# A new written order and engine choice for a linear-attention and feed-forward kernel

## The chip, the cores and the metric

The kernel runs on one core of a Trainium2 chip. A core has a matrix engine (TensorE, PE in the profile), three engines for elementwise work (VectorE or DVE, ScalarE or ACT, GpSimd or POOL), a queue engine (SyncE or SP) that issues all of this kernel's data transfers, and sixteen DMA engines that carry them out. The engines run at the same time, each works through its own instructions in order, and they wait for one another by semaphores. The metric is the device time of one execution in microseconds; less is better.

## The reference

The inputs r, k, v, w have 4 batches, 8 heads, 768 steps and 48 elements per head, in float32. For each batch and head a state S of 48 x 48 is carried along the steps:

```
y[t] = r[t] . (S + (u * k[t]) v[t]^T)
S    = diag(w[t]) S + k[t] v[t]^T
```

The outputs y, put together over the heads, are 3072 tokens of 384 elements. A feed-forward block follows: h = x @ w_in (384 x 2048), g = s * relu(h)^2 + b, out = g @ w_out (2048 x 384), in float32.

## The kernel before

The steps are cut into 24 chunks n of 128 steps (six per batch). Within a chunk the recurrence is written as matrix products. With the running sum of log w (a product with a triangular matrix), r and k are scaled by its exponentials; then the chunk's own part is a masked 128 x 128 product per head, and the part from earlier chunks a product with the carried state. The first four chunks are "packed": two neighbouring chunks of a batch are loaded together and take several smaller products each. Two chunks make one tile T of 256 tokens for the feed-forward block, twelve tiles in all.

Each piece of work is an operation with a short name. n is a chunk, T a tile, i a part.

| name | engine | what it does (line) |
|---|---|---|
| load n.x, li, lo, load_u, small | SP | loads of w, r, k, v (x = 0 to 3; L296, packed L304), of the pieces of w_in and w_out (L719, L729), of u, s, b |
| ln, exp, exn | ACT | log of w; exponentials of the running sums, E (L317, L413, L428) |
| cum, inc | PE, DVE | running sums into a PSUM tile cums (L372 to L397), and inc = cums + log w (L418) |
| mul | DVE | prd = r, k times E (L437, L444) |
| tr, tev | PE, ACT | transposes of prd and their copy RK to SBUF (L471, L491); for chunks 9 and up tev is a DMA transpose on SP (L501) |
| mt, msk | PE, DVE | K R^T of two chunks in four PSUM buffers (L531, L543), masked into mt_sb, two msk a chunk (L555) |
| rkp, rku, cd, yd | POOL, DVE for cd | the u term: r*k, times u, summed per head, times v (L322, L328, L345, L351) |
| vb | POOL or ACT | v to bfloat16 (L870, L872) |
| ymm, yev | PE, DVE | y of the chunk (L574 to L606), plus yd, into x_sb (L651) |
| dmm, sup, l2, st | PE, DVE, POOL | the state's update (L625, L638, L671, L679, L458, L688) |
| xtr, xev | PE, ACT | x transposed, copied into the tile's xT (L699, L714) |
| g1 T.i, relu, sq | PE, ACT, DVE or ACT | an eighth of h (six matmuls, L749), relu (L762), square into gT (L772 on ACT, L774 on DVE) |
| g2 T.i, oev, store | PE, DVE, SP | four matmuls into the output tile o_ps (L793), times s plus the b term (L804), store (L823) |
| ci, co, csred, csadd, cssplit, csspread, csevac | several | weights to bfloat16 (ci, co: L870 on ACT, L874 on DVE, L872 on POOL); column sums of w_out for the b term |
| u_mm, u_ev | PE, DVE | u spread over the partitions (L893, L897) |
| +N | PE | N matmuls on a constant tile, whose result is not used (L1119) |

Nothing is scheduled by a framework. The text ORDER lists all operations once, and the last loop of the kernel emits them in this order. Each engine's queue is ORDER's words for that engine, in their sequence. A suffix picks the engine where there is a choice: @A is ACT, @D is DVE, @P is POOL.

```
for o in pl.order(ORDER):
    if isinstance(o, int):
        warm(o)
    else:
        o["fn"](*o["args"])
```

The method order (L138) checks that each operation comes after those it needs and after the last user of the buffer that it takes. The planned durations given to add (the third argument) are read by a search that is not part of the kernel; they decide nothing when the kernel is built.

Buffers are taken in rings, in ORDER's sequence. PSUM has six buffers "P", which cum, tr, mt (four at once), ymm, xtr, dmm and g1 take in turn, and two buffers "o" for o_ps: the output tile that comes next but one waits until oev has read the earlier one. The w_in and w_out pieces share four staging buffers: a lo waits for the ci that has read its buffer.

Of the kernel before, what the change touches and what calls it, by code (L numbers as in the profile page):

```python
# [1159 lines left out]
```

## Time and profile before

| what | value |
|---|---|
| median of 13 runs | 186.88 us (185.64 to 195.22) |
| profiled execution | 185.64 us, its span 183.6 us |
| PE busy | 176.3 us, 96% of the span |
| DVE busy | 140.4 us, 77% |
| ACT busy | 146.5 us, 80% |
| POOL busy | 104.7 us, 57% |
| mean granted clock of TensorE | 0.999 |
| first g1 starts | 20.89 us |
| last matmul ends | 180.4 us |
| g1 matmuls (L749) | 576, 71.9 us |
| g2 matmuls (L793) | 400, 72.8 us |

The span reaches from the first to the last instruction; the run's time holds some more around it. Busy times add up an engine's instructions without the overlaps, so a share of 96% means that PE has 7.3 us without a matmul. In a timeline line the first number is the start, the second the time until the last instruction of the line ends, then engine, line, operation, the tiles, their shapes and the number of instructions; a bracket tells how long the engine was idle before it and whose end it waited for. Matmuls of one line overlap, and so do neighbouring instructions of DVE and ACT, so that costs in a queue are better read from start to start.

### The profile page before, as it was taken

What the parts mean: (1) busy time and instruction counts of PE and PEld (TensorE: products, weight loads), DVE (VectorE), ACT (ScalarE), POOL (GpSimd) and SP (SyncE); (2) the same over time, 40 slices, a digit from 0 to 9 for tenths busy, and PEclk for the clock granted to TensorE, in tenths of its full rate; (3) what the DMA queues carried; (4) which work ended last, traced back from release to release, by engine and by line L of the source; (5) the groups of instructions that cost most, each with busy time, mean ns of one, the idle gap of its engine ahead of it and who ended that gap; (6) DMA issues with size and microseconds to landing.
All of it is one profiled execution on the core that took longest, in us unless ns stands there. A gap on an engine that the chain in (4) does not pass through costs nothing.

```text
span 183.6 us, 5087 instructions
## 1 busy us (share of the span) xinstructions
PE 176.3 (96%) x1994; PEld 139.5 (76%) x1994; DVE 140.4 (77%) x250; ACT 146.5 (80%) x286; POOL 104.7 (57%) x139
## 2 busy tenths in 40 slices
PE   7999899999998999997999999999999999999993
PEld 4568798866786787785788878877886978888672
DVE  7659899998969979859978698697898959522231
ACT  3588999999989999887878979878989677754900
POOL 3685930019988999698397299194495493100000
PEclk9999999999999999999999999999999999999999
DMA  6999989589989989999699989999994890004022
GB/s 162 324 312 345 407 294 327 116 154 230 217 174 210 219 181 215 201 238 151 127 221 188 188 201 185 202 234 192 199 193 97 191 190 4 2 5 171 0 86 86
DMA packets 113449, 34.14 MB, mean 186 GB/s; under 512 B 108177, under 2 KB 111378, under 8 KB 113426
## 3 DMA queue, kind: packets, MB, share of 16 engines
q1 hardware_dynamic: 113426, 33.83, 80.6%
q8 instruction: 15, 0.25, 0.6%
q14 instruction: 8, 0.07, 0.1%
HBM read 25.17 MB, written 4.72 MB: 163 GB/s over the span
## 4 chain that ended last, share of the span: by engine, by line
PE 47%; ACT 3%; DVE 2%; issue 0%; ACTq 0%
PE o_ps L793 21%; PE h_ps L749 19%; PE mt_ps L543 2%; DVE mt_sb L555 2%; PE y_ps L606 1%; ACT rh L762 1%; PE xt_ps L699 1%; PE y_ps L597 1%; ACT gT L772 1%; PE d_ps L638 1%; PE cums L391 1%; DVE o_sb L804 1%; ACT E L428 0%; ACT xT L714 0%; DVE inc L418 0%; ACT E L413 0%
## 5 line engine op out<-in xcount | busy, mean ns | idle before, releaser
L793 PE MATMUL o_ps<-w_out,gT 128*128 128x384 bf16 (+1 forms) x400 | 72.8, 320 | 1.5 <-DVE gT L774 0.9
L749 PE MATMUL h_ps<-xT,w_in 128*128 128x256 bf16 x576 | 71.9, 273 | 0.2
L762 ACT ACTIVATE rh<-h_ps 128x512 bf16<-128x512 f32 x96 | 55.4, 599 | 14.2 <-PE h_ps L749 13.0
L749 PEld LDWEIGHTS <-w_in 128*128 128x128 bf16 x576 | 61.8, 114 | 4.3 <-issue 0.2
L793 PEld LDWEIGHTS <-gT 128*128 128x128 bf16 x400 | 36.6, 98 | 19.1 <-DVE gT L774 1.5
L772 ACT ACTIVATE gT<-rh 128x512 bf16<-128x512 bf16 x69 | 42.3, 633 | 0.3
L351 POOL TENSOR_TENSOR yd<-vt,cd 128x384 bf16<-128x384 f32 x20 | 19.0, 954 | 17.1 <-DVE cd L345 17.1
L555 DVE TENSOR_TENSOR mt_sb<-mt_ps,tri_strict 128x512 bf16<-128x512 f32 x40 | 25.3, 680 | 2.7 <-PE mt_ps L543 2.7
L328 POOL TENSOR_TENSOR rku<-rkp,u_bc 128x384 f32<-128x384 f32 x24 | 24.2, 1008 | 0.7
L322 POOL TENSOR_TENSOR rkp<-rkt 128x384 f32<-128x384 f32 x20 | 23.9, 1198 | 0.9 <-DMA rkt<-in_k_dram 0.9
L804 DVE SCALAR_TENSOR_TENSOR o_sb<-o_ps,s_bc,bconst 128x384 f32<-128x384 f32 (+1 forms) x25 | 14.8, 594 | 11.7 <-PE o_ps L793 11.7
L774 DVE TENSOR_TENSOR gT<-rh 128x512 bf16<-128x512 bf16 x27 | 15.7, 590 | 9.2 <-ACT rh L762 9.1
L444 DVE TENSOR_TENSOR prd<-rkt,E 128x768 bf16<-128x768 f32 x20 | 22.1, 1108 | 0.1
L413 ACT ACTIVATE E<-cums 128x388 f32<-128x388 f32 (+1 forms) x32 | 15.7, 496 | 6.2 <-DVE inc L418 3.3
L688 POOL TENSOR_TENSOR st<-stmp,l 128x384 bf16<-128x384 bf16 x16 | 15.6, 979 | 6.4 <-DVE stmp L679 6.4
L872 POOL CAST vb<-vt 128x384 bf16<-128x384 f32 x12 | 7.4, 624 | 17.9 <-DMA vt<-in_v_dram 17.9
L651 DVE TENSOR_TENSOR x_sb<-y_ps,yd 128x384 bf16<-128x384 f32 x24 | 13.0, 551 | 3.7 <-PE y_ps L606 2.1
L345 DVE TENSOR_REDUCE cd<-rku 128x8 f32<-128x384 f32 x24 | 12.9, 543 | 1.6 <-POOL rku L328 1.6
L714 ACT COPY xT<-xt_ps 128x384 bf16<-128x384 bf16 x24 | 11.0, 482 | 2.3 <-PE xt_ps L699 2.2
L418 DVE TENSOR_TENSOR inc<-cums,logw 128x384 f32<-128x384 f32 x16 | 8.8, 549 | 4.2 <-ACT E L413 3.4
L317 ACT ACTIVATE logw<-wt 128x384 bf16<-128x384 f32 x20 | 10.5, 523 | 0.2 <-DMA wt<-in_w_dram 0.2
L679 DVE TENSOR_TENSOR stmp<-d_ps,st 128x384 bf16<-128x384 f32 x16 | 8.7, 549 | 2.0 <-PE d_ps L638 1.6
(94 smaller groups left out, 198.9 us busy)
## 6 DMA issues: line engine op xcount, KB each, us to landing
out_dram<-o_sb SPq DMA_DIRECT2D x23, 192.0 KB, 2.7
wt<-in_w_dram SPq DMA_DIRECT2D x20, 192.0 KB, 3.8
rkt<-in_r_dram SPq DMA_DIRECT2D x20, 192.0 KB, 4.1
rkt<-in_k_dram SPq DMA_DIRECT2D x20, 192.0 KB, 3.7
vt<-in_v_dram SPq DMA_DIRECT2D x20, 192.0 KB, 3.8
wi_st<-in_moe_w_in_dram SPq DMA_DIRECT2D x4, 768.0 KB, 9.0
wo_st<-in_moe_w_out_dram SPq DMA_DIRECT2D x4, 768.0 KB, 7.2
pkt<-in_w_dram SPq DMA_DIRECT2D x2, 384.0 KB, 4.1
```

The source lines that it names most:

```text
L322: nc.gpsimd.tensor_tensor(out=rkp, in0=c["r"], in1=c["k"], op=ALU.mult)
L328: nc.gpsimd.tensor_tensor(out=rku.rearrange("t h d -> t (h d)"), in0=c["rkp"].rearrange("t h d -> t (h d)"), in1=u_bc, op=ALU.mult,)
L351: nc.gpsimd.tensor_tensor(out=yd, in0=c["v"], in1=c["cd"].unsqueeze(2).to_broadcast([128, H, D]), op=ALU.mult,)
L413: nc.scalar.activation(out=c["E"][:, x, 0:w], in_=ps[:, 0:w], func=AF.Exp)
L444: nc.vector.tensor_tensor(out=prd[:, :, :, 0:D], in0=c["rk"], in1=c["E"][:, :, 0:HD].rearrange("t x (h d) -> t x h d", h=H), op=ALU.mult,)
L555: nc.vector.tensor_tensor(out=c["mt"][:, sg], in0=c["mt_ps"][sg], in1=(masks[:, n % 2] if packed(n) else tri_strict) .unsqueeze(1) .to_bro ...
L749: nc.tensor.matmul(ps[:, f, :], lhsT=w_in_sb[ft // FPP][:, kt, :].rearrange("p (m j) -> p j m", j=FPP)[:, ft % FPP, :], rhs=xT[T][:, kt, : ...
L762: nc.scalar.activation(out=rh, in_=hs[T, i], func=AF.Relu)
L772: nc.scalar.activation(out=g, in_=rh, func=AF.Square)
L774: nc.vector.tensor_tensor(out=g, in0=rh, in1=rh, op=ALU.mult)
L793: nc.tensor.matmul(os_[T, k][:, cols], lhsT=gT[T][:, ft, tt * 128 : (tt + 1) * 128], rhs=w_out_sb[ft // FPP][:, ft % FPP, cols], start=(ft ...
L804: nc.vector.scalar_tensor_tensor(out=o_sb[:, cols], in0=os_.pop((T, k))[:, cols], scalar=s_bc, in1=bconst[:, cols], op0=ALU.mult, op1=ALU.add,
```

## The change

The whole text ORDER is replaced by another order of the same operations. It holds 40 of the unused matmuls instead of 38. Some operations stand on other engines: among the weight casts, ci1 moves from ACT to DVE and ci2 from DVE to POOL; vb4, vb5 and vb7 move from POOL to ACT, vb9, vb10 and vb13 from ACT to POOL; 70 of the 96 squares are on ACT instead of 69. The planned cost of u_mm is 0.85 instead of 0.7; the search that made the new order also counted the instruction fetches as work of the DMA engines, and let only one engine at a time read a PSUM tile. No function, shape, buffer count or dependency changes.

```
--- before.py
+++ after.py
 ORDER = """
-load0.0 load0.1 load_u ln0 ln1 +16 cum0.0 cum0.1 cum1.0 exp0.0 load0.2 exp0.1 mul0.0 mul0.1 exp1.0
-load0.3 mul1.0 cum1.1 load2.0 load2.2 load2.3 u_mm tr0 exp1.1 mul1.1 +2 tr1 u_ev tev0 tev1 +9 mt0
-vb0@P load4.0 l20 rkp0 rku0 load2.1 rkp1 l21 msk0.0 msk1.0 vb1@A ln2 msk0.1 rku1 li0 ln3 cd0 +4
-cum2.0 exp2.0 dmm0 cum3.0 msk1.1 cum3.1 ln4 vb2@A cum2.1 sup0 exp3.0 exp2.1 vb3@A st0 +1 cum4.0 li1
-exp3.1 l22 yd0 mul2.0 mul2.1 exp4.0 mul3.0 ymm0 cd1 mul3.1 yd1 ymm1 dmm1 tr2 sup1 rkp2 l23 ci0@A
-yev0 dmm2 tev2 tr3 li2 rku2 sup2 yev1 xtr0 tev3 cd2 +5 xtr1 l24 rkp3 xev0 rku3 yd2 xev1 +1 mt2 g10.0
-ci1@A msk2.0 st2 msk2.1 msk3.0 li3 g10.1 relu0.1 msk3.1 relu0.0 dmm3 g10.2 g10.3 relu0.2 lo0 ymm2
-ci2@D cd3 ymm3 lo1 st1 yd3 lo2 sup3 yev2 cum4.1 xtr2 ci3@A relu0.3 g10.4 load5.0 sq0.0@D lo3 load5.1
-yev3 load6.0 load4.1 sq0.3@A g10.5 co0@D load4.2 xev2 xtr3 load5.2 csred0@D sq0.2@A sq0.1@A relu0.4
-g10.6 xev3 exp4.1 small2 g20.4 g20.0 g10.7 load4.3 g11.0 g11.1 co1@D relu0.5 g11.2 sq0.5@A relu0.7
-relu0.6 sq0.4@D sq0.7@A csred1@D sq0.6@A ln5 small g11.3 relu1.0 vb4@P load5.3 rkp4 csadd1@D relu1.2
-relu1.3 g20.1 g11.4 cum5.0 relu1.1 exp5.0 co2@D csred2@D g20.5 cum5.1 exp5.1 sq1.2@A csadd2@D
-load6.1 load6.2 g11.5 co3@D sq1.0@D g11.6 csred3@D csadd3@D load7.0 cssplit g11.7 g20.2 g20.6 g20.3
-rku4 mul4 relu1.4 load8.0 sq1.3@A ln6 load9.0 relu1.6 relu1.7 sq1.1@A cum6.1 g20.7 relu1.5 csspread
-load6.3 mul5 tr4 cum6.0 load7.1 tr5 csevac sq1.5@A l25 oev0.1 oev0.0 exp6.0 tev5 exp6.1 dmm4 g21.4
-g21.0 tev4 g21.1 g21.5 vb5@P sup4 sq1.4@A cd4 dmm5 mul6 mt4 rkp5 load7.2 ln7 load7.3 g21.6 sup5
...
-rkp7 sup6 exn8 load10.1 g12.1 inc9 exp9.0 oev1.1 relu2.0 sq2.0@A g12.2 relu2.1 dmm7 tr7 rku7 g12.3
-tev7 relu2.2 rkp6 sq2.1@D oev1.0 load11.3 vb8@P cd7 sup7 mul8 load9.2 g12.4 g22.0 relu2.3 relu2.4
...
-g14.1 g14.2 g14.3 cd10 relu4.0 exp13.0 inc13 sup11 mul12 l212 cd11 oev3.0 relu4.1 yd10 vb12@P mt10
-relu4.2 g14.4 g23.7 relu4.3 sq4.0@D sq4.1@A load13.3 load14.1 exn13 st10 load13.2 msk10.0 msk11.0
-load15.0 oev3.1 rkp12 l213 msk10.1 relu4.4 ln14 g14.5 store2.0 load16.0 g24.4 st11 msk11.1 sq4.2@A
-cum14.0 g24.0 dmm12 rku12 sq4.4@A g14.6 yd11 sup12 mul13 ymm10 ymm11 yev10 ln15 rkp13 relu4.5
-exp14.0 sq4.3@A load15.3 yev11 relu4.6 sq4.5@A vb13@A g14.7 g24.1 g24.5 rku13 tev12 load14.2 inc14
...
-relu7.7 sq7.7@A store5.1 relu8.0 mt18 tev20 exn21 msk19.0 relu8.1 msk18.0 msk18.1 yd19 g27.6 g18.2
-ln22 msk19.1 g18.3 cum22.0 dmm18 g27.2 sq8.1@A ln23 inc22 mul21 g27.3 ymm19 g18.4 g27.7 relu8.3
-relu8.2 rkp20 sq8.0@A load22.2 g18.5 tev21 sq8.3@A yev19 relu8.4 exp22.0 rku20 yd18 vb21@P rkp21
-sup18 relu8.5 ymm18 xtr19 rku21 st18 sq8.2@A exn22 cum23.0 sq8.4@D g18.6 oev7.1 yev18 oev7.0 xtr18
-g18.7 g28.0 inc23 store7.0 relu8.6 g28.4 load20.3 g28.5 cd21 xev18 exp23.0 xev19 supn21 supn20
-sq8.5@A relu8.7 load23.2 mt20 store6.1 g19.0 mul22 g19.1 g28.1 msk20.0 msk20.1 msk21.0 yd21 msk21.1
...
-relu11.3 sq11.2@A sq11.0@A relu11.6 store9.1 g210.5 relu11.7 g210.0 g210.6 g210.7 store8.1 store9.0
-g210.1 relu11.4 sq11.3@A g210.2 store8.0 sq11.6@D sq11.7@D oev10.1 g210.3 sq11.4@D g211.8 g211.0
-g211.1 oev10.0 store10.1 g211.2 g211.4 g211.3 g211.5 g211.6 g211.7 g211.9 g211.10 g211.11 oev11.0
-oev11.1 oev11.2 store10.0 store11.1 store11.0 store11.2
+load0.0 ln0 ln1 +17 cum0.0 load0.1 load0.2 load_u cum1.0 cum0.1 exp0.0 rkp0 u_mm cum1.1 load0.3
+mul0.0 load2.3 exp1.0 exp0.1 l20 vb1@A exp1.1 load2.2 load2.0 mul0.1 mul1.0 load2.1 +4 tr0 load4.0
+mul1.1 +5 tr1 u_ev l21 tev0 vb0@P rku0 tev1 dmm0 +5 mt0 ln2 cd0 sup0 msk1.0 ln3 vb3@A rkp1 yd0 rku1
+li0 +1 cum2.0 cum3.0 st0 msk0.0 msk1.1 msk0.1 rkp3 exp2.0 mul2.0 l22 cum2.1 +5 cum3.1 ln4 ymm0 cd1
+exp2.1 exp3.0 exp3.1 ci0@A yd1 mul2.1 yev0 cum4.0 vb2@A ymm1 xtr0 xev0 li2 mul3.0 exp4.0 tr2 tev2
+li1 mul3.1 +2 dmm2 yev1 li3 lo0 dmm1 xtr1 xev1 sup2 tr3 sup1 +1 g10.0 ci2@P tev3 g10.1 mt2 load5.0
+ci1@D relu0.0 lo1 relu0.1 g10.2 rku3 g10.3 cd3 sq0.0@A sq0.1@A lo2 relu0.2 relu0.3 ci3@A st2 msk2.0
+lo3 g10.4 msk2.1 small2 msk3.0 l24 relu0.4 rkp2 cum4.1 load6.0 g10.5 msk3.1 ymm3 load4.1 rku2 ymm2
+sq0.3@D cd2 st1 yd3 yev3 yd2 co0@D l23 xtr3 yev2 g10.6 csred0@D load4.2 exp4.1 relu0.5 ln5 g20.4
+cum5.0 load5.1 sq0.2@A xtr2 relu0.6 xev2 co1@D load5.2 g10.7 xev3 csred1@D rkp5 small g20.0 g11.0
+load6.1 exp5.0 sq0.4@A g11.1 sq0.5@A relu0.7 rkp4 g11.2 cum5.1 g11.3 sq0.6@A csadd1@D co2@D load6.2
+relu1.0 relu1.1 csred2@D load4.3 g20.5 g20.1 relu1.2 sq0.7@A sq1.2@A exp5.1 csadd2@D co3@D csred3@D
+g20.6 csadd3@D g20.2 g11.4 g20.7 g11.5 cssplit load5.3 load7.0 g11.6 relu1.3 rku4 sq1.0@A sq1.3@A
+ln6 sq1.1@A mul4 relu1.4 relu1.5 sq1.5@D mul5 g20.3 cum6.0 relu1.6 csspread load8.0 cum6.1 csevac
+exp6.0 dmm3 tr4 g11.7 tr5 exp6.1 tev4 tev5 load6.3 oev0.1 g21.0 vb4@A sq1.4@A oev0.0 load9.0 sup3
+relu1.7 g21.4 rku5 vb5@A sq1.6@A load7.1 load8.1 ln7 mt4 mul6 g21.1 l25 g21.5 dmm4 g21.6 load7.2
...
+g12.2 oev1.0 rku6 sq2.0@A mul7 g12.3 oev1.1 rkp7 sup6 relu2.1 sq2.1@D tr7 cum9.0 rku7 inc9 vb7@A cd6
+load10.0 dmm7 st6 relu2.3 relu2.2 tev7 exp9.0 sup7 mul8 cd7 g12.4 relu2.4 g22.0 g12.5 mt6 msk6.0
...
+load13.3 g23.3 oev3.0 g14.0 g14.1 relu4.0 mt10 sq4.0@A relu4.1 g14.2 load15.3 relu4.2 load15.1
+load14.1 yd10 msk10.0 rkp11 rku11 l212 rkp13 rku13 msk10.1 cd11 msk11.0 g14.3 cum13.0 g14.4 msk11.1
+exp13.0 load14.2 sq4.1@A relu4.3 inc13 g23.7 load12.3 yd11 ymm10 g24.0 oev3.1 g14.5 ymm11 yev10
+store2.0 load17.0 sq4.3@A ln14 load15.2 relu4.4 exn13 relu4.5 sq4.2@A g14.6 xtr10 relu4.6 xev10
+yev11 sq4.4@D mul12 xtr11 xev11 g14.7 g24.1 relu4.7 g24.4 rkp12 cum14.0 g24.5 vb13@P tev12 ln15
...
+load19.0 load17.3 g25.6 sup15 yev13 cd15 xtr13 cd14 dmm14 sup14 mt14 msk14.0 xev13 msk14.1 st15 st14
+yd15 yd14 g25.3 g16.0 g16.1 relu6.0 g16.2 g16.3 msk15.0 load17.1 relu6.1 msk15.1 ymm14 ymm15 sq6.0@D
+l216 rkp16 ln18 relu6.2 mul16 g16.4 vb16@P g16.5 yev15 yev14 relu6.3 xtr15 cum18.0 g25.7 oev5.0
...
+g18.6 inc22 sq8.4@A mul21 sq8.3@D mt18 tev21 exn22 st19 rku19 load21.3 store6.1 g28.5 sq8.5@A g28.1
+supn21 cd19 msk19.0 g28.6 msk18.0 relu8.6 g18.7 sq8.6@A msk18.1 ln23 ymm18 msk19.1 yd19 rkp21 yev18
+relu8.7 ymm19 vb20@P cum23.0 g28.2 yd20 rku21 inc23 yev19 mt20 cd21 xtr19 store7.1 store6.0 load22.1
+load23.1 load22.2 load23.2 msk20.0 msk21.0 sq8.7@A store7.0 load22.3 yd21 vb21@P st18 exp23.0 xtr18
+msk20.1 supn20 g28.7 msk21.1 xev18 g28.3 vb22@P xev19 g19.0 rkp23 exn23 ymm20 g19.1 relu9.0 sq9.0@D
+g19.2 relu9.1 relu9.2 g19.3 rku23 g19.4 ymm21 yev20 rkp22 oev8.1 sq9.2@D mul22 g19.5 xtr20 relu9.4
...
+xev22 xev23 sq10.4@A g210.0 g210.1 g111.0 g111.1 g111.2 sq10.5@D relu10.7 sq10.7@A relu11.0 g111.3
+oev9.1 g111.4 g111.5 g210.4 store9.0 relu11.1 g111.6 sq10.6@D sq11.1@D g111.7 sq11.0@A g210.2 g210.5
+g210.3 relu11.4 relu11.3 relu11.6 relu11.7 sq11.4@A relu11.5 sq11.3@A store8.1 sq11.7@D oev10.0
+relu11.2 g210.6 g210.7 g211.4 sq11.6@A oev10.1 sq11.5@A sq11.2@A g211.0 g211.8 g211.1 g211.5
+store10.1 store9.1 g211.6 g211.7 store10.0 g211.2 g211.3 oev11.1 g211.9 store11.1 oev11.0 g211.10
+g211.11 oev11.2 store11.0 store11.2
...
-    add("u_mm", "PE", 0.7, spread_u, (), ["load_u"], [("o", ["u_ev"])], 2.0, lat=0.2)
+    add("u_mm", "PE", 0.85, spread_u, (), ["load_u"], [("o", ["u_ev"])], 2.0, lat=0.2)
```

## The prediction

> **What bounds the kernel now.** I read the page first: the busy shares, then the chain that ended last, then TensorE's (PE's) own timeline for every idle gap, and last the other engines' timelines around those gaps.
>
> ```profile
> span 183.6 us, 5087 instructions
> ...
> PE 176.3 (96%) x1994; PEld 139.5 (76%) x1994; DVE 140.4 (77%) x250; ACT 146.5 (80%) x286; POOL 104.7 (57%) x139
> ...
> PE 47%; ACT 3%; DVE 2%; issue 0%; ACTq 0%
> ```
>
> PE is idle for 183.6 - 176.3 = 7.3 us. The change removes no PE work, so these 7.3 us, the warm-up matmuls and the start, where PE waits for a chain through all engines, are all that it can move. The mean granted clock is 0.999, so it enters no term.
>
> ```profile
> 10.82 0.64 PE L531 MATMUL mt_ps<-RK 48*64 48x128 bf16 x32 [0.37 <-ACT RK L491]
> 20.13 0.64 PE L531 MATMUL mt_ps<-RK 48*64 48x128 bf16 x32 [0.47 <-ACT RK L491]
> ...
> 55.62 0.50 PE L793 MATMUL o_ps<-w_out,gT 128*128 128x384 bf16 x2 [0.53 <-DVE gT L774]
> 83.81 0.82 PE L793 MATMUL o_ps<-w_out,gT 128*128 128x384 bf16 x4 [0.33 <-DVE gT L774]
> 85.53 0.81 PE L793 MATMUL o_ps<-w_out,gT 128*128 128x384 bf16 x4 [0.66 <-DVE o_sb L804]
> 139.28 0.34 PE L699 MATMUL xt_ps<-identity,x_sb 128*128 128x128 bf16 x3 [0.30 <-ACT E L428]
> ```
>
> The bracket is PE's idle time and what ended it. From 42 us to the last matmul at 180.4 the four lower gaps, 1.82 us, are nearly all of PE's idle time. About 3.2 us lie behind the last matmul.
>
> **The change, part by part.** Its one number, the planned cost of u_mm, is read by nothing that emits instructions: nothing. The rest is a new order. I follow it by the rows: PE costs start to start are 0.66 us for a g1 (six matmuls), 0.65 for a g2, 0.45 for a tr, 0.55 for mt, 0.37 for ymm (0.17 + 0.20), 0.17 for xtr; DVE costs start to start are 0.60 for a msk (2.40 for the four from 20.58 to 22.98), 0.47 for yev, 0.9 for mul.
>
> *Warm-ups.* 40 instead of 38. The first sixteen take 3.60 us, 0.225 each; a 17th moves cum0.0 from 4.82 to 4.88. The others stand in waits that stay: within the next item.
>
> *Start, to 42 us.* cum1.0 before cum0.1 puts exp0.1 one exp (0.49 us) later, and vb1 stands on ACT before exp1.1; so mul1.1 ends near 9.3 instead of 8.9, and tev1 near 11.05 instead of 10.77. mt0 starts at about 11.1 instead of 10.82. But sup0 now runs on DVE before the four msk, so they end near 14.35 (before 14.28), and ymm0 starts at 14.8 in both. Then w_in's first piece decides:
>
> ```profile
> 16.78 1.47 ACT L870 CAST w_in<-wi_st 128x1536 bf16<-128x1536 f32 x1 [0.50 <-DMA wi_st<-in_moe_w_in_dram]
> 18.16 1.92 ACT L491 COPY RK<-trps 128x1024 bf16<-128x1024 bf16 x2
> ...
> 22.98 1.48 DVE L874 CAST w_in<-wi_st 128x1536 bf16<-128x1536 f32 x1
> ```
>
> Its load is issued tenth in both, so ci0 stays at 16.78. Behind it ACT now has vb2, xev0, exp4.0, tev2, xev1 (0.45 + 0.45 + 0.45 + 0.95 + 0.4): g10.0 starts near 20.9, as now (20.89). mt2, however, ran before g10.0 and now runs after g10.1, near 22.2 instead of 20.13: 0.55 us of PE work is still owed, and the msk of chunks 2 and 3 start near 23.05 instead of 20.58. Against these 2.5 us, DVE has 2.6 us less between there and mul5: one weight cast (start to start 1.40; it comes earlier now), one sup and one sq. DVE is busy without a gap there (20 to 41 us), and tr5 waits for its mul5. Those msk end near 25.5, ymm3 at 26.55, and yev3 starts at 26.7; summing the new queue from there through four weight casts, csred, csadd and cssplit, mul5 ends near 42.05 instead of 41.46. The PE work done by the end of tr5 is the same set in both orders. I take +0.5. Bounds: -0.3 if mt0's lateness vanishes in the waits, +1.6 by the cast of the next paragraph.
>
> *ci2 on GpSimd.* This form, 128x1536 to bf16, has no POOL row. POOL cast 128x384 in 0.51 at 43.97 and, beside VectorE, in 1.04 at 40.79; four times as much is 2.0 and 4.2. Its piece lands at 18.8 (issued 11.3, 7.5 to landing), rku3 (1.0) follows, and DVE wants cd3 at 22.55: up to 2.6 us cost nothing. I take 2.0, the undisturbed row; 4.2 makes DVE, and so PE, 1.6 late. [...]
>
> *vb4 and vb5 from GpSimd to ACT.* Now POOL waits for this load, at no cost:
>
> ```profile
> 40.79 1.04 POOL L872 CAST vb<-vt 128x384 bf16<-128x384 f32 x1 [14.96 <-DMA vt<-in_v_dram]
> ...
> 25.60 2.05 SPq L729 DMA_DIRECT2D wo_st<-in_moe_w_out_dram x1
> 31.57 2.55 SPq L296 DMA_DIRECT2D rkt<-in_r_dram  x1
> 37.60 0.43 SPq L296 DMA_DIRECT2D vt<-in_v_dram  x1
> ```
>
> In the new order ACT waits instead, with sq1.4, relu1.7 and, behind them, g21.2 queued. On SP, load4.3 moves behind load6.1 and load6.2: between lo3 and it stand nine issues instead of six, two of them more loads of 192 KB and one tiny. Two loads cost 2.0 us at 1.0 each (the spacing past 48 us) to 3.3 at 1.65 (27.70 to 37.60 for six). lo3, waiting for ci3, is up to 0.8 later. Landing then lies between 42.8 and 44.9, and ACT asks near 43.95, after tev5. So 0 to 0.95; I take 0.3, nearer to the spacing of the busy stretch only by a part, because small issues are among the six.
>
> *The four gaps.* (a) 55.62: g22.0 waited for sq2.1 on DVE, recorded at 1.25 us beside GpSimd against 0.41 at 25.77. The old order leaves only g12.4 (0.66) between sq2.1 and g22.0; the new one leaves tr7, cum9.0, dmm7 and g12.4, 1.5 us. Gone: -0.53. (b) 83.81: g24.4 waited for sq4.0 on DVE; sq4.0 is now on ACT, right behind its relu, and g24.4 comes after g14.7: -0.33. (c) 85.53: g24.0 waited for the second o buffer, whose reader oev3.1 stood behind two msk. The new g24.0 comes first and takes oev3.0's buffer, and g24.4 with the other comes three g1 and a g2 later: -0.66. (d) 139.28: xtr18 waited for yev18, which stood on DVE behind a slow sq8.4 (1.25 at 136.99, beside GpSimd) and oev7.1; now neither stands between ymm18 and yev18, and five other PE operations stand between ymm18 and xtr18: -0.30. Together -1.82.
>
> *What is late next.* ymm20: behind mt20 stand two xtr, g28.7, g28.3 and g19.0, 2.3 us, but its third msk comes after cd21: 0.15 + 0.46 + 1.80 + 0.10 = 2.5, so +0.2. mt4: tev4 and tev5 end near 43.95, PE is there at 43.85: +0.1. xtr15: DVE has the four msk, sq6.0 and mul16 before yev15, 0.15 + 2.40 + 1.25 + 0.95 = 4.75 us behind mt14 even with sq at its slowest, and PE comes to xtr15 5.3 us behind mt14: just in time, 0. I add 0.05 for smaller ones. Not found ones: 0 to 1.8, as many as now.
>
> *The shared PSUM tile.* exp and inc of a chunk read one cums tile, and each waits for the other:
>
> ```profile
> DVE inc L418 <- ACT E L413: 3.4, 3, 2.4
> ACT E L413 <- DVE inc L418: 3.3, 5, 1.3
> ```
>
> These 6.7 us are on DVE and ACT; none of PE's gaps names DVE's inc, and the one that names an exp's line (139.28) was a wait for yev18. The new order may shorten them, which is worth nothing more here. The Trainium skill (PSUM — Partial Sum Buffer, section "PSUM bank collisions raise a hardware error") says that two engines, readers too, must be kept off one bank and its quadrant. By that a wait of about one read stays in each of the sixteen chunks whatever the order; charged to PE in full it would leave nothing to gain here either, so the sum is the same by the rule and by the trace.
>
> *End.* oev11.2 (0.42) and its store (issued 180.9, span ends 183.6) stay behind the same last three g2. store11.0 goes out a little earlier, before a store that waits for oev11.2 anyway: 0. ACT's new order ends with sq11.2: seven instructions behind relu11.7 (0.15 + 0.5 + 7 x 0.55), about 4.6 us after g111.7's last matmul, when PE, with five g2, a half, a g2 and a half done, reaches g211.1 (3.25 + 0.33 + 0.65 + 0.33 = 4.56): +0.05.
>
> **Sum.** 0.5 + 0.3 - 1.82 + 0.35 + 0.05 = -0.6 us: span 183.0. The profiled execution took 185.64, 2.04 more than its span, the lowest of the 13 runs; their median, 186.88, lies 1.24 above it. I carry the difference over: 186.88 - 0.6 = 186.3.
>
> **Rivals.**
> 1. *All the gaps go and the start costs nothing* (the planner now knows what it mispriced). -1.82 - 0.3 = -2.1: 184.8. For it: each gap has a named cause that the new order takes away. Against: mt2 and load4.3 are plainly later.
> 2. *As many new gaps as old.* PE has little slack at 96%, and sq took 0.41 to 1.25 us by chance of what GpSimd does. -0.6 + 1.5 = +0.9: 187.8. Against: the sites I followed leave 1.3 us or more.
> 3. *Slower: ACT waits at vb4.* If all nine SP issues go at 1.65 us from 28.4 (lo3's end, 0.8 later), load4.3 is issued at 43.3 and lands 3.2 later (40.79 - 37.60), at 46.5: 2.5 us of ACT, which is busy 9.2 of 10 us there, and so of PE. Instead of my 0.3: -0.6 + 2.2 = +1.6: 188.5. It decides from a landing of about 44.9 on. Against: the page shows the DMAs past 41 us at 1.0 us a load.
> 4. *The order makes no difference:* PE's work is fixed, gaps move only: 186.9.
>
> **How the numbers follow.** A measurement of this kernel can tell about 0.5%, 0.93 us: faster is below 185.95, slower above 187.81. My sum 0.36, within 0.9 us to either side, and about a third of it below 185.95; rival 1 0.22; rival 2 0.15, half of it above 187.81; rival 3 0.19; rival 4 0.08. Faster 0.12 + 0.22 = 0.34, slower 0.08 + 0.19 = 0.27 and 0.04 more for the upper GpSimd cast, same the rest. The range goes from rival 1 to just short of rival 3's end, which leaves half of each outside, 0.2: 184.8 to 188.4; my own case's is 185.4 to 187.2.
>
> **What would show it.** PE without a gap at g22.0, g24.4, g24.0 and xtr18; g10.0 at 20.9 and mt2 behind two g1; tr5 ending near 42.6 instead of 42.1; POOL's cast of w_in at 2.0 us; ACT's idle before vb4, by DMA, under 1 us. Wrong: an ACT gap of over 1 us before vb4, a POOL cast over 2.6 us, or PE idle by more than 1 us between 50 and 160 us.

## The result and the profile after

The changed kernel takes 189.54 us (median of 11 runs, 188.73 to 191.11) against 186.89 us (48 runs): a ratio of 1.0178, 95% interval 1.0150 to 1.0207. The ratio leaves out executions of the kernel before that fell into a slower state of the chip, so it is not the quotient of the two medians. The changed kernel is slower by 1.8%. The prediction was 186.3 us in a range of 184.8 to 188.4, so it was wrong, by 1.1 us beyond its upper end. The profiled execution took 188.37 us, less than any of the 11 runs, with a span of 186.6 us, 3.0 us longer than the 183.6 of before.

The page of the changed kernel: span, busy shares, and the first line of the chain.

```profile
span 186.6 us, 5099 instructions
...
PE 176.5 (95%) x1996; PEld 139.6 (75%) x1996; DVE 143.8 (77%) x249; ACT 146.1 (78%) x286; POOL 108.5 (58%) x140
...
PE 65%; DVE 9%; ACT 2%; issue 2%; DVEq 0%; ACTq 0%
```

PE's work is the same (176.5 against 176.3 us). Its idle time went from 7.3 to 10.1 us, and DVE's part of the chain from 2 to 9%. PE's timeline (start, duration, operation, and in the bracket the idle time ahead of it with what ended it) says where:

```profile
19.05 0.69 PE L625 MATMUL d_ps<-vb,prd 64*128 64x96 bf16 x16 [0.83 <-ACT vb L870]
21.10 1.47 PE L749 MATMUL h_ps<-xT,w_in 128*128 128x256 bf16 x12 [0.54 <-ACT xT L714]
...
37.48 0.81 PE L793 MATMUL o_ps<-w_out,gT 128*128 128x384 bf16 x4 [0.27 <-DVE w_out L874]
...
42.76 0.32 PE L849 MATMUL csb_ps<-cs_sum,ones 128*128 128x384 bf16 x1 [2.27 <-DVE cs_sum L841]
43.35 0.32 PE L849 MATMUL csb_ps<-cs_sum,ones 128*128 128x384 bf16 x1 [0.27 <-DVE cs_sum L842]
...
52.80 0.34 PE L699 MATMUL xt_ps<-identity,x_sb 128*128 128x128 bf16 x3 [0.26 <-DVE x_sb L651]
...
100.81 0.81 PE L793 MATMUL o_ps<-w_out,gT 128*128 128x384 bf16 x4 [0.56 <-DVE o_sb L804]
...
132.23 0.81 PE L749 MATMUL h_ps<-xT,w_in 128*128 128x256 bf16 x6 [0.24 <-ACT xT L714]
```

The four old gaps (55.62, 83.81, 85.53, 139.28) are gone. The large new one is 2.54 us at csspread, where PE waits for cssplit on DVE. The balance of the two spans closes: 2.54 here, 0.35 more at the start (0.83 + 0.54 against the old 0.18 + 0.37 + 0.47), 1.33 of small new gaps, 0.4 behind the last matmul, 0.2 of PE work, minus the old 1.82: +3.0 us.

Why was cssplit late? The same instructions on DVE's timeline, first in the kernel before, then in the changed one:

```profile
36.61 1.54 DVE L831 TENSOR_TENSOR wo_st<-wo_st 128x768 f32<-128x768 f32 x2
38.18 0.56 DVE L838 TENSOR_TENSOR wo_st<-wo_st 128x384 f32<-128x384 f32 x1
38.77 0.36 DVE L841 CAST cs_sum<-wo_st 128x384 bf16<-128x384 f32 x1
```

```profile
36.48 0.95 DVE L874 CAST w_out<-wo_st 128x1536 bf16<-128x1536 f32 x1
37.52 2.85 DVE L831 TENSOR_TENSOR wo_st<-wo_st 128x768 f32<-128x768 f32 x2
40.40 1.24 DVE L838 TENSOR_TENSOR wo_st<-wo_st 128x384 f32<-128x384 f32 x1
41.67 1.03 DVE L841 CAST cs_sum<-wo_st 128x384 bf16<-128x384 f32 x1
```

The three last lines have the same shapes and data as before and take 2.66 us longer (5.12 against 2.46). GpSimd's timeline in the changed kernel shows what is new beside them:

```profile
36.46 3.50 POOL L322 TENSOR_TENSOR rkp<-rkt 128x384 f32<-128x384 f32 x2 [7.86 <-DMA rkt<-in_k_dram]
40.03 2.46 POOL L328 TENSOR_TENSOR rku<-rkp,u_bc 128x384 f32<-128x384 f32 x2
```

In the kernel before, GpSimd was idle from 25.8 to 40.79, because vb4 stood at the head of its queue and waited for its load: the 14.96 us that the prediction shows at that cast. This wait, called the shelter below, kept GpSimd's work away from DVE's block. With vb4 on ACT, rkp5, rkp4 and the rku start as soon as the k pieces land, and these were also issued earlier (from 29.63 us instead of 34.17), so the work runs beside DVE's block. It is slowed too (1.75 us for each rkp and 1.23 for each rku instead of 1.00). Not every meeting slows DVE: the cast at 36.48 kept its 0.95 us, while rkp5, which had started 0.02 us ahead of it, took 1.82.

### The profile page after: what moved, and what is told of

The parts are those of the page before. It is cut to its first block, busy times and chain, and to the rows that moved or that the text cites. A ratio compares the mean times of both kernels' runs of the same rounds, so it can differ in the third digit from the quotient of the medians.

```text
span 186.6 us, 5099 instructions
## 1 busy us (share of the span) xinstructions
PE 176.5 (95%) x1996; PEld 139.6 (75%) x1996; DVE 143.8 (77%) x249; ACT 146.1 (78%) x286; POOL 108.5 (58%) x140
## 4 chain that ended last, share of the span: by engine, by line
PE 65%; DVE 9%; ACT 2%; issue 2%; DVEq 0%; ACTq 0%
PE o_ps L793 27%; PE h_ps L749 25%; PE mt_ps L543 3%; DVE prd L444 2%; PE xt_ps L699 2%; PE y_ps L606 2%; PE y_ps L597 2%; DVE wo_st L831 2%; PE d_ps L638 1%; PE cums L391 1%; PE trps L471 1%; DVE gT L774 1%; DVE o_sb L804 1%; ACT xT L714 1%; DVE wo_st L838 1%
## 5 line engine op out<-in xcount | busy, mean ns | idle before, releaser
L749 PE MATMUL h_ps<-xT,w_in 128*128 128x256 bf16 x576 | 72.9, 273 | 0.8 <-ACT xT L714 0.8
L322 POOL TENSOR_TENSOR rkp<-rkt 128x384 f32<-128x384 f32 x20 | 25.6, 1281 | 10.3 <-DMA rkt<-in_k_dram 8.6
L328 POOL TENSOR_TENSOR rku<-rkp,u_bc 128x384 f32<-128x384 f32 x24 | 26.0, 1090 | 1.1 <-DVE u_bc L897 0.3
L351 POOL TENSOR_TENSOR yd<-vt,cd 128x384 bf16<-128x384 f32 x20 | 16.5, 832 | 13.1 <-DVE cd L345 12.1
L774 DVE TENSOR_TENSOR gT<-rh 128x512 bf16<-128x512 bf16 x26 | 14.6, 572 | 9.6 <-ACT rh L762 9.5
L688 POOL TENSOR_TENSOR st<-stmp,l 128x384 bf16<-128x384 bf16 x16 | 15.0, 937 | 10.1 <-DVE stmp L679 7.5
L458 POOL TENSOR_TENSOR l<-E,par 128x8 f32<-128x8 f32 x20 | 8.5, 428 | 6.7 <-ACT E L413 6.7
```

Source lines behind the costliest of these rows:

```text
L322: nc.gpsimd.tensor_tensor(out=rkp, in0=c["r"], in1=c["k"], op=ALU.mult)
L328: nc.gpsimd.tensor_tensor(out=rku.rearrange("t h d -> t (h d)"), in0=c["rkp"].rearrange("t h d -> t (h d)"), in1=u_bc, op=ALU.mult,)
L351: nc.gpsimd.tensor_tensor(out=yd, in0=c["v"], in1=c["cd"].unsqueeze(2).to_broadcast([128, H, D]), op=ALU.mult,)
L749: nc.tensor.matmul(ps[:, f, :], lhsT=w_in_sb[ft // FPP][:, kt, :].rearrange("p (m j) -> p j m", j=FPP)[:, ft % FPP, :], rhs=xT[T][:, kt, : ...
L774: nc.vector.tensor_tensor(out=g, in0=rh, in1=rh, op=ALU.mult)
```

## The experiments

Theory T1: GpSimd's released work slows DVE, DVE's cssplit comes late, and PE waits. Rivals: R1, csspread's place in PE's queue costs the time; R2, not GpSimd but the earlier loads; R4, the start. All ratios are to the kernel before, run on the same chip in the same session, with the 95% interval in parentheses; differences to the changed kernel are between medians of different sessions.

**1. Take the shelter from the kernel before.** Only GpSimd's queue is reordered.

```
-... relu1.0 vb4@P load5.3 rkp4 ...  rku4 ...  rkp5 ...
+... relu1.0 rkp5 rkp4 rku4 vb4@P load5.3 ...
```

> Edit: the kernel before, in which only GpSimd's queue is reordered: rkp5, rkp4 and rku4 stand ahead of vb4, whose load lands at 40.79, instead of behind it. So POOL no longer waits for that load with this work behind it. T1: rkp5 and rkp4 start when their k pieces have landed, near 37.5 to 38.5, beside csred3's second half, csadd3, cssplit and mul4; DVE's instructions there grow towards those of the changed kernel (csadd3 from 0.56 to about 1.2, cssplit's cast from 0.36 to about 1.0), mul5 ends 0.8 to 2.0 us later than 41.46, tr5 waits for it, and the time rises by 0.7 to 2.0 us, to 187.6 - 188.9. R1 and R2 (GpSimd beside DVE costs nothing): DVE's durations and the time stay as before, 186.9.

Measured 189.88 us, 1.0182 (1.0103 to 1.0262): the kernel before with one queue of an off-path engine reordered loses as much as the changed kernel. DVE's timeline, then GpSimd's, then PE's:

```profile
40.02 1.24 DVE L844 TENSOR_TENSOR cs_sum<-wo_st,cs_sum 128x384 bf16<-128x384 f32 x1
41.19 3.41 DVE L446 TENSOR_TENSOR prd<-rkt,E 128x768 bf16<-128x768 f32 x2
44.52 1.13 DVE L806 SCALAR_TENSOR_TENSOR o_sb<-o_ps,s_bc,bconst 128x384 f32<-128x384 f32 x2
```

```profile
39.66 2.46 POOL L324 TENSOR_TENSOR rkp<-rkt 128x384 f32<-128x384 f32 x2 [13.51 <-DMA rkt<-in_k_dram]
42.20 1.59 POOL L330 TENSOR_TENSOR rku<-rkp,u_bc 128x384 f32<-128x384 f32 x1
43.73 1.23 POOL L874 CAST vb<-vt 128x384 bf16<-128x384 f32 x1
```

```profile
42.99 0.62 PE L473 MATMUL trps<-identity,prd 128*128 128x128 bf16 x8 [1.35 <-DVE prd L446]
44.66 0.62 PE L473 MATMUL trps<-identity,prd 128*128 128x128 bf16 x8 [0.81 <-DVE prd L446]
```

GpSimd came 1.2 to 2.2 us later than expected and met other instructions: mul4 and mul5, 3.41 us instead of 1.82. Two instructions that read one operand from PSUM kept their time: o_sb at 44.52 took 1.13 us, its first 0.4 beside the cast, and in the kernel before 1.14 us beside rkp4, which kept its 1.00. Not all of this execution's loss is GpSimd's: its span is 2.5 us above that of before, and 0.84 of it is a longer wait at mt2 (1.31 us instead of 0.47), which the traces of run 3 and of run 8's second kernel, with the same start, show too (1.20 and 1.23). R1 and R2 expected no change and fall: neither csspread nor a load was moved.

**2. Hold GpSimd back in the changed kernel.**

```
-... csred1@D rkp5 small ... relu0.7 rkp4 g11.2 ... cssplit load5.3 ...
+... csred1@D small ... relu0.7 g11.2 ... cssplit rkp5 rkp4 load5.3 ...
+        if n == 5:                       # in pool1, ahead of the multiplication
+            mark = const.tile([128, 8], FP32, name="mark", tag="mark")
+            nc.gpsimd.tensor_copy(out=mark, in_=cs_sum[:, 1, 0:8])
```

> Edit: the changed kernel, in which GpSimd (POOL) is made to read eight columns of cs_sum ahead of rkp5, so that rkp5, rkp4 and the rku behind them start only when VectorE (DVE) has finished cssplit; nothing else is moved. Theory T1 (GpSimd's rkp5, rkp4, rku4, rku5 beside csred3, csadd3 and cssplit slow DVE, and PE waits for cssplit at csspread): csred3 returns from 2.85 us for its two instructions to about 1.55, csadd3 from 1.24 to 0.56, the cast from 1.03 to 0.36, so cssplit ends about 2.65 us earlier, near 40.7; PE's wait of 2.27 + 0.27 us at csspread goes, and the time falls by 2.0 to 2.6 us, to 187.0 - 187.6. A little may come back as slower mul4 and mul5 beside the moved work. Rival R1 (the place of csspread in PE's queue, or the later start, is what costs, and DVE's durations are the weight casts' own): the durations stay within 0.2 us of the changed kernel's, the wait at csspread stays, time 189.3 - 189.8. Rival R2 (what matters is the SP and DMA traffic of the earlier loads at that moment, not GpSimd): DVE's instructions stay long although POOL is idle beside them.

187.69 us, 1.0086 (1.0042 to 1.0130), 1.85 us below the changed kernel. On DVE's timeline every duration up to cssplit is back:

```profile
39.81 1.55 DVE L837 TENSOR_TENSOR wo_st<-wo_st 128x768 f32<-128x768 f32 x2
41.40 0.56 DVE L844 TENSOR_TENSOR wo_st<-wo_st 128x384 f32<-128x384 f32 x1
41.99 0.36 DVE L847 CAST cs_sum<-wo_st 128x384 bf16<-128x384 f32 x1
...
44.07 1.76 DVE L450 TENSOR_TENSOR prd<-rkt,E 128x768 bf16<-128x768 f32 x1
```

The wait at csspread is gone. Two things are not as expected: mul5 now meets the released rkp5 (1.76 us, and PE waits 0.74 for it), and the block ends at 42.9 instead of 40.7, because this execution was already 2.3 us late at g10.0 (23.36 against 21.10). Runs 6 and 7 come back to that.

**3. The price by itself.** The kernel before, with twelve more multiplications ahead of vb4; their product is not used.

```
+            c["pre"] = work.tile([128, H, D], FP32, name="rkp", tag="rkp", bufs=2)
+            for _ in range(12):
+                nc.gpsimd.tensor_tensor(out=c["pre"]..., in0=u_bc, in1=u_bc, op=ALU.mult)
```

> Edit: the kernel before with twelve more GpSimd multiplications of 128x384 fp32 (1.00 us each alone) in front of vb4, where GpSimd has nothing to do from 25.8 to 40.8; their product is overwritten unused. It gives the price of the suspected cause by itself. T1: DVE's tensor_tensor instructions with two fp32 inputs and its 384-wide casts take about 1.8 to 3 times as long wherever they meet one of them (csred pairs 1.55 to about 2.9, csadd 0.56 to about 1.2), and DVE is some 4 to 7 us late at mul5, most of which PE shows as a wait there. The rival that GpSimd does not slow DVE: durations as before, and the twelve instructions end near 38 without a change of the time.

196.52 us in its one run. DVE's timeline, then GpSimd's:

```profile
33.52 2.68 DVE L839 TENSOR_TENSOR wo_st<-wo_st 128x768 f32<-128x768 f32 x2
36.23 1.07 DVE L846 TENSOR_TENSOR wo_st<-wo_st 128x384 f32<-128x384 f32 x1
37.22 1.58 DVE L882 CAST w_out<-wo_st 128x1536 bf16<-128x1536 f32 x1
...
43.76 1.22 DVE L782 TENSOR_TENSOR gT<-rh 128x512 bf16<-128x512 bf16 x1
```

```profile
25.91 15.06 POOL L344 TENSOR_TENSOR rkp<-u_bc 128x384 f32<-128x384 f32 x12
```

The csred pair goes from 1.55 to 2.68 us, csadd from 0.56 to 1.07, the large cast from 0.95 to 1.58, sq from 0.42 to 1.22; GpSimd's own twelve take 15.06 instead of 12. DVE's mul5 ends near 51.3 instead of 41.5, later than expected (4 to 7 us): vb4, rkp4 and rku4 start nearly when they do in the kernel before (40.92, 41.72 and 43.10 instead of 40.79, 41.79 and 42.87), and DVE, late by then, meets them and what follows them too. The Trainium skill (SBUF — State Buffer, section "Who interferes with whom") says that a VectorE instruction with two SBUF inputs contends with a GpSimd instruction that reads SBUF, and one with at most one does not, outside the 2-port modes. The rows with two inputs agree, and so does o_sb in run 1; the casts have one SBUF input and were slowed as well, and no row shows in which mode they ran. The rows add the size: 1.7 to 2.9 times here.

**4. Is it the place in PE's queue?**

```
-... relu1.6 csspread load8.0 cum6.1 csevac exp6.0 dmm3 tr4 g11.7 tr5 exp6.1 ...
+... relu1.6 load8.0 cum6.1 exp6.0 dmm3 tr4 g11.7 tr5 csspread csevac exp6.1 ...
```

> Edit: the changed kernel with csspread and csevac moved behind tr5 in the order, so that PE no longer stands at csspread while cssplit is late; DVE and POOL keep their queues. T1: mul4 and mul5 stand behind cssplit on DVE's own queue and still end near 44.2 and 45.4, so the wait only moves from csspread to tr4 and tr5 (PE has cum6.1 and dmm3, some 0.7 us, to do in between): the time falls by 0 to 0.6 us, 188.9 - 189.5. R1 (head of the line: it is csspread's place in PE's queue): PE does not wait any more, and the time falls by 2.0 to 2.5 us, to 187.0 - 187.5.

191.95 us, 1.0311 (1.0181 to 1.0442): R1 falls, and T1's number was wrong too, by 2.4 us. PE's timeline, and two rows of its windows (the third column from the end is the granted clock):

```profile
43.90 0.68 PE L474 MATMUL trps<-identity,prd 128*128 128x128 bf16 x8 [3.11 <-DVE prd L447]
...
48.68 1.46 PE L796 MATMUL o_ps<-w_out,gT 128*128 128x384 bf16 x8 [1.32 <-DVE o_sb L807]
```

```profile
44.00:46.00 2.00, 2.00 (x18) 1.63 (x18) 1.04 (x2) 0.43 (x1) 0.59 (x1) 0.58 1.05 206
46.00:48.00 2.00, 1.35 (x9) 0.81 (x8) 0.00 (x0) 0.61 (x2) 0.00 (x0) 0.57 1.13 222
```

The stall moved to tr4 as T1 says. But it became 3.11 us in one piece, and over the 4 us behind it the clock was granted at 0.58 and 0.57 (1.00 in the changed kernel's profiled execution); then the later csspread made oev0.1 late, another 1.32.

**5. Is it the order on DVE?** mul4 and mul5 ahead of csred3, tr4 and tr5 ahead of csspread.

```
-... co3@D csred3@D ... cssplit ... mul4 relu1.4 relu1.5 sq1.5@D mul5 ... csspread ... tr4 g11.7 tr5 ...
+... co3@D mul4 mul5 csred3@D ... cssplit ... sq1.5@D ... tr4 tr5 csspread ...
```

> Edit: the changed kernel with mul4 and mul5 moved ahead of csred3 on DVE, and tr4 and tr5 ahead of csspread on PE; GpSimd's queue as in the changed kernel. T1: GpSimd's rkp and rku still run beside DVE and DVE's block is as slow as in the changed kernel (csred3 above 2 us), but only csspread and csevac, wanted by oev0.1, come behind it. tr4 and tr5 start when mul4 and mul5 are done near 40 instead of 44.2 and 45.4. csspread then waits less than 1 us, and the time falls by 1.0 to 2.5 us, 187.0 - 188.5. If cssplit, now about 2 us later, makes oev0.1 late and PE waits for the o buffers, the gain is given back: 189 - 190. R1: as T1's first case, since PE has other work at the head of its queue.

190.94 us, 1.0261 (1.0176 to 1.0345): no gain; its median lies 1.4 us above the changed kernel's. DVE's timeline, then PE's:

```profile
37.87 3.44 DVE L447 TENSOR_TENSOR prd<-rkt,E 128x768 bf16<-128x768 f32 x2
41.22 3.01 DVE L834 TENSOR_TENSOR wo_st<-wo_st 128x768 f32<-128x768 f32 x2
```

```profile
45.28 1.06 PE L852 MATMUL csb_ps<-cs_sum,ones 128*128 128x384 bf16 x2 [3.30 <-DVE cs_sum L844]
```

Whatever DVE does in that stretch pays: now mul4 and mul5 take 3.44 and csred3 still 3.01, and csspread waits 3.30 us. From 44 to 50 us the clock was granted at 0.50; it had fallen before the wait ended at 45.28. The Trainium skill (TensorE: Matmul & The Clock Gate, section "HAM oscillation — how this bites in real kernels") warns of PE idle gaps above about 3.4 us; here it fell at shorter ones, 3.11 us in run 4 and 3.30 in this run, and the measurement decides.

**6. Hold GpSimd until mul5.** As in 2, but rkp5, rkp4 and rku4 stand behind mul5, and the marker reads mul5's prd.

> Edit: as the run with GpSimd held until cssplit (187.69 us, 1.0086 of the kernel before), but rkp5, rkp4 and rku4 now wait for mul5 instead. There PE still stood 0.74 us at tr5, because mul5 ran beside the released rkp5 and took 1.76 us instead of 0.95. T1: mul5 returns to 0.95, the 0.74 us at tr5 go, and the time is 186.8 - 187.3, if rkp4, rku4 and what waits for them (cd4, yd4, the first ymm of the tile) are not late by then. If they are, POOL's 4 us of work, which now begin near 45 instead of 43, show as a PE wait at ymm4 or xtr4, and the time is 187.7 - 188.7. A rival in which PE's stall has nothing to do with GpSimd leaves 187.7.

187.18 us, 1.0041 (1.0010 to 1.0072), as expected; PE waits for nothing between 40 and 50 us. But the start was late again (g10.0 at 23.39), with the DMAs moving 262 GB/s from 4 to 16 us, where the changed kernel's moved about 322. Both runs had one thing in common: the 32 bytes a partition of the marker's tile, which move every buffer allocated behind it. In both executions the clock, too, was low in the start: at 0.50 from 9 to 11 us in run 2, and here (third column from the end):

```profile
8.00:12.00 4.00, 4.00 (x20) 2.22 (x19) 2.69 (x4) 1.46 (x3) 2.64 (x5) 0.50 1.27 261
```

**7. Take the tile away; and give it to the kernel before.** The marker is written into rkp, which rkp5 overwrites:

```
-            nc.gpsimd.tensor_copy(out=mark, in_=...)
+            nc.gpsimd.tensor_copy(out=rkp[:, 0, 0:8], in_=cb[5]["prd"][:, 0, 0, 0:8])
```

> Edit: as the run with GpSimd held until mul5 (187.18 us, 1.0041), but the marker is written into the rkp tile, which rkp5 overwrites right behind it, and not into a tile of 32 bytes a partition of its own. That extra tile moved all buffers allocated behind it by 32 bytes, and in both runs that had it the DMAs of the first 16 us moved 262 GB/s instead of 322 (changed kernel), and g10.0 started at 23.4 instead of 21.1. Theory L (the 32 bytes slow the DMAs' writes): the rate returns to 320 or so, g10.0 to 21.1, and with T1's undisturbed DVE the span is 182.7 - 183.5: 184.7 - 185.5 us, 1.2 to 2.3 us faster than the run with the tile, a ratio of 0.988 to 0.995 to the kernel before. If the slow start was chance or belongs to the held GpSimd, the time stays at 187.0 - 187.4. If PE has another stall instead (cd4, yd4 late, as mul5 now ends earlier than the data), 185.5 - 186.5.

185.44 us, 0.9946 (0.9912 to 0.9979). This kernel beats both, the kernel before by little. From 4 to 16 us its DMAs moved 315, 279 and 296 GB/s (321, 325 and 337 in its repeat, below), and g10.0 starts at 21.36. Its page, and PE's timeline from 22 us to the end, all gaps above 0.2 us:

```profile
span 183.4 us, 5100 instructions
```

```profile
37.69 0.81 PE L798 MATMUL o_ps<-w_out,gT 128*128 128x384 bf16 x4 [0.23 <-DVE w_out L879]
...
50.80 0.34 PE L704 MATMUL xt_ps<-identity,x_sb 128*128 128x128 bf16 x3 [0.69 <-DVE x_sb L656]
```

The counterpart is the kernel before with the unused tile:

```
+    mark = const.tile([128, 8], FP32, name="mark", tag="mark")      # behind u_bc
```

> Edit: the kernel before with one more tile of 128x8 fp32 (32 bytes a partition) allocated behind u_bc and never used. Theory L: the DMAs of the first 16 us fall from about 320 to about 262 GB/s, the weights' first piece lands some 1.5 to 2.5 us later, and the time rises by 1 to 2.5 us, a ratio of 1.005 to 1.013. Rival (chance): no change, 1.000 within 0.003.

189.28 us, 1.0129 (1.0059 to 1.0199). The page's row of the DMA queue (packets, MB, share of time), and PE's timeline:

```profile
q1 hardware_dynamic: 113426, 33.83, 89.9%
```

```profile
22.74 0.64 PE L534 MATMUL mt_ps<-RK 48*64 48x128 bf16 x32 [0.51 <-ACT RK L494]
44.40 0.62 PE L474 MATMUL trps<-identity,prd 128*128 128x128 bf16 x8 [1.17 <-DVE prd L447]
46.07 0.62 PE L474 MATMUL trps<-identity,prd 128*128 128x128 bf16 x8 [0.81 <-DVE prd L447]
```

The same packets and bytes took 89.9% of the engines' time instead of 80.6%, and the rate from 4 to 16 us was 261 to 266 GB/s instead of 312 to 324. mt2 came 2.6 us late and DVE's block 2.7, while vb4's load came only 1.0 later: mul4 and mul5 met GpSimd (3.42 us), and PE waited 1.98 us for them, part of the 1.3%. The clock was at 1.00 throughout, so the slower start does not need the low clock of runs 2 and 6. These two carried a loss that had nothing to do with their question.

**8. Where else the new order loses: the start, and the part behind 50 us.**

```
start:  the changed order up to xev3, then that of before (vb4@P ahead of rkp4)
rest:   the order of before up to g12.0, then the changed one
```

> Edit: the order of the changed kernel up to xev3 (near 29 us), and from there that of the kernel before, with vb4 on GpSimd ahead of rkp4; exp5.0 some places earlier for the turn of a PSUM buffer. It measures the start alone, which the prediction put at +0.5 us. T1: GpSimd waits for vb4's load again, DVE's last part runs at its undisturbed durations, and the time is 0.3 to 0.8 above the kernel before: 1.002 to 1.004. If load4.3 lands earlier than the 40.79 of the kernel before (the changed start issues its loads some 2 us earlier), rkp4 runs beside csadd3, cssplit and mul4, and 0.5 to 1.5 more come on top: 1.005 to 1.012. Rival R4 (the start itself is what costs): 1.015 or more, with DVE's durations undisturbed.

191.98 us, 1.0292 (1.0236 to 1.0348). It did not isolate the start. GpSimd's timeline, then DVE's:

```profile
38.13 1.24 POOL L874 CAST vb<-vt 128x384 bf16<-128x384 f32 x1 [9.82 <-DMA vt<-in_v_dram]
```

```profile
38.06 1.73 DVE L833 TENSOR_TENSOR wo_st<-wo_st 128x768 f32<-128x768 f32 x2
39.82 1.24 DVE L840 TENSOR_TENSOR wo_st<-wo_st 128x384 f32<-128x384 f32 x1
...
42.96 3.42 DVE L446 TENSOR_TENSOR prd<-rkt,E 128x768 bf16<-128x768 f32 x2
```

The load landed at 38.13 instead of 40.79, the shelter ended 2.7 us earlier, DVE's block stood 1.45 us later, and csadd3, cssplit, mul4 and mul5 met GpSimd. PE's waits add to 4.0 us, and the clock was at 0.50 from 47 to 49 us. The direction is the one expected for an early landing, the size is twice that. Leaving vb4 on GpSimd does not keep the shelter by itself, then: an earlier load ends it too. R4 asked for undisturbed durations on DVE, which this run does not have, so the start itself stays unmeasured by it.

> Edit: the order of the kernel before up to g12.0 (near 50 us), and from there the order of the changed kernel; exp9.0 and inc9 a few places earlier, so that each PSUM buffer's turn is kept. T1: the new order's loss lies wholly ahead of 50 us. This kernel keeps the start and the sheltered GpSimd of the kernel before and gets the four vanished gaps: -1.82 for these, +0.56 for the changed kernel's wait at 100.81, +0.2 to 0.4 for its end: -0.9 to -1.1 us, a ratio of 0.994 to 0.995. Rival R3 (the new order is also worse behind 50 us, in ways that the one trace does not show, or its gaps come and go by chance): 0.998 to 1.005.

This second kernel gave 186.60 us, 1.0004 (0.9962 to 1.0047): rival R3, by which the new order gains nothing behind 50 us. The order behind 50 us is not worth 0.5% by itself. Its trace shows why; PE's timeline, then DVE's:

```profile
57.63 0.50 PE L795 MATMUL o_ps<-w_out,gT 128*128 128x384 bf16 x2 [0.92 <-DVE gT L776]
...
99.69 0.81 PE L795 MATMUL o_ps<-w_out,gT 128*128 128x384 bf16 x4 [0.52 <-DVE o_sb L806]
```

```profile
56.33 1.25 DVE L776 TENSOR_TENSOR gT<-rh 128x512 bf16<-128x512 bf16 x1
```

Gap (a), the wait of g22.0 for sq2.1, is back, larger than before, though the words behind g12.0 are the changed kernel's: sq2.1 again ran beside an rku, and cum9.0, which covered it on PE, was already done.

**9. The last wait, and the winner again.** Two kernels: that of run 7 with one more edit (GpSimd does rkp4, rku4 ahead of rkp5 and yd4 ahead of st3, DVE does yev4 ahead of sup5), and that of run 7 unchanged.

> Edit: the run with GpSimd held and no extra tile (185.44 us, 0.9946), in which PE's only wait of more than 0.25 us behind 40 us is 0.69 at xtr4, for yev4. GpSimd now does rkp4, rku4 ahead of rkp5, and yd4 ahead of st3; DVE does yev4 ahead of sup5. yev4 could start 0.44 to 0.7 earlier. If that wait was the last one there, the time falls by 0.3 to 0.6 us against the same run repeated beside it; if another comes out behind it (ymm5's msk, xtr5) by 0 to 0.2. It is at the limit of what the comparison can tell.

> Edit: none; the run with GpSimd held and no extra tile once more, beside the one above. 185.2 - 185.7 us, a ratio of 0.991 to 0.997 to the kernel before.

The repeat gave 185.85 us, 0.9966 (0.9936 to 0.9996): the gain over the kernel before is there twice, some 0.3 to 0.5%. The edit gave 186.39 us, 0.9999 (0.9972 to 1.0026): its wait at xtr4 fell from 0.69 to 0.26, and the time did not (in its profiled execution the clock was at 0.50 from 16 to 18 us). In both executions a wait at the same place stood again near 99 us (0.61 and 0.65, for o_sb), which the first execution of the winner did not have. Gaps of half a microsecond come and go between executions of one kernel.

## Why the prediction was wrong

By its own steps, against the changed kernel's profiled execution:

- **The start: +0.5.** About right. g10.0 at 21.10 (20.9 was said), mt2 at 22.50 behind two g1 (22.2), 0.35 us more of idle. The cast ci0, said to stay at 16.78, started at 17.11, and dmm2's wait of 0.83 for vb2 was not foreseen.
- **"Summing the new queue from there through four weight casts, csred, csadd and cssplit, mul5 ends near 42.05". This step failed.** The queue was the right one: from yev3's start to mul5's end it held 15.35 us by the prediction, and 15.6 us (27.32 to 42.93) in the run with GpSimd held. In the changed kernel it took 18.3 (27.06 to 45.37). The durations were rows of the kernel before, measured while GpSimd was idle beside them, and the change took that idleness away.
- **"Now POOL waits for this load, at no cost".** True for POOL, and the place where the miss could have been seen. The prediction followed the wait to its new engine (rival 3: ACT) and not to what it left behind: rkp5, rkp4 and two rku, 4 us of two-input work, free to start when the k pieces landed, with csred3 to mul5 running then. The text even has sq "recorded at 1.25 us beside GpSimd against 0.41", and used that only at the gaps.
- **vb4 on ACT: +0.3.** It was 0: ACT came to vb4 at 46.99, directly behind tev5 and without waiting for the load. load4.3 was issued at 35.51, 2.1 us earlier than before and not later, as the prediction had it. Rival 3, the slower case, fell with it. The forecast held a chance of 0.31 for slower, for another mechanism, and its range ended just short of rival 3's 188.5.
- **ci2 on GpSimd: 2.0 us.** 1.46 us, less than four times the narrower cast. It changed nothing.
- **The four gaps: -1.82.** All four went, as said, but 1.33 us of small ones came where 0.35 was counted: rival 2 in part. Run 8 shows that the cover at gap (a) was thin.
- **The end: +0.05.** It was 0.4. The prediction had store11.0 go "a little earlier"; in the new order oev11.0 is second, 1.0 us ahead of oev11.2 instead of 2.0, and the span ends 3.2 us behind oev11.2's end instead of 2.8. This is read from the two traces; no run tried it.

With GpSimd held until mul5 and no extra tile, the span is 183.4 and 184.3 us in two executions; the prediction's sum was 183.0. The changed kernel's 186.6 is 3.6 us above it: the missing term, one wait of 2.54 us, and beside it 1.0 of small gaps, 0.35 at the end and 0.2 of PE work, less 0.45 that vb4 and the start did not cost. This is the account of the fastest of its twelve executions; none of the others was traced.

## What to carry to other kernels

An idle engine off the critical path can be a shelter for its neighbour: before an instruction that waits at the head of such a queue is moved away, or its load made earlier, list what stands behind it, when its data land, and which instructions of the neighbour will run then. A duration taken from a profile holds for the neighbours that it had there; VectorE work with two SBUF inputs had two prices here, with and without GpSimd. To hold an engine back, a tiny read of the result that must come first was enough here, but it should be written into a buffer that exists already.

## What the runs showed of the hardware

- VectorE beside GpSimd (alone, then beside): two fp32 inputs of 768 in pairs 1.55 to 2.57 - 3.01 us, of 384 0.56 to 1.07 - 1.24, the cast of 384 0.36 to 1.03, of 1536 0.95 to 1.58 - 1.75 (but 0.95 once, at 36.48 in the changed kernel), bf16 squares 0.41 to 1.05 - 1.25; GpSimd's multiplication 1.00 to 1.19 - 1.82. Both sides are slowed.
- With 32 bytes a partition of an unused tile the DMAs of the start moved 262 instead of about 320 GB/s, and the kernel before took 1.3% longer (run 7); part of that is PE's wait of 1.98 us for DVE beside GpSimd. The addresses themselves were not looked at, and other offsets were not tried.
- The granted clock fell to 0.50 at PE waits of 3.11, 3.30 and 3.58 us (runs 4, 5 and 3), and in run 8's first kernel behind four waits of 0.60 to 1.35 us within 5 us. It also fell in the starts of three executions (run 2, run 6 and the edit of run 9), where PE's longest wait since the first matmul had been 0.22, 0.67 and 0.88 us. So no bound on a single wait comes out of these runs.
- In the changed kernel, with a stall of 2.54 us, the profiled execution kept 0.998, while eight of its twelve executions show a mean of 0.98 to 0.991. A mean of 0.991 or less also stands in four of six executions of run 2, six of ten of run 6, one and three of twelve of run 7 and its repeat, and six of twelve of the edit of run 9, none of which has the stall in its trace. So the stall at csspread need not be what lowers it in those eight; no trace was taken of one of them. Nor does the lower clock account for the loss: the other four executions, at 0.998 or 0.999, took 188.37 to 190.68 us, those eight 188.73 to 191.11.
